# Weight folding in a four-layer attention kernel: 32-row block transposes through DRAM in place of TensorE transposes, rests gathered, weight reloads ordered behind a branch

## The chip, the cores and the metric

The kernel runs on one core of one Trainium2 chip. Its time is the device time of one execution in microseconds; of several executions the median counts. The profile shown is of one such execution.

## The reference, cut to what matters

Two kinds of layer alternate twice (A, B, A, B) on 2048 tokens of width D = 576 with 32 heads of 18. The same weights serve both rounds.

```python
def _A_ref(x, wq, wk, wv, wo):            # 32 query heads, one key and value head
    q = (x @ wq).reshape(B, S, H, Dh).transpose(0, 2, 1, 3)
    k = x @ wk; v = x @ wv
    p = softmax(einsum("bhqd,bkd->bhqk", q, k) * (Dh ** -0.5))
    return einsum("bhqk,bkd->bhqd", p, v) ... @ wo
def _B_ref(x, wqkv, w_phi, wo):           # linear attention
    q, k, v = (x @ wqkv) split
    pq = einsum("bhsd,hdf->bhsf", q, w_phi); pk = the same of k
    phi = concat(softmax(p), softmax(-p))            # for q and for k
    o = phi_q (phi_k^T v) / (phi_q sum(phi_k))
    return o ... @ wo
x = x + A(layernorm(x)); x = x + B(layernorm(x)); and both once more
```

`x @ wqkv` followed by the per-head product with `w_phi` is a product with a weight that can be worked out once: for queries and for keys, wq' = wq·blockdiag(w_phi). Working this out is called **folding** here.

## The kernel before, in words

One program does two rounds, "layer 0" and "layer 1", each an A and a B. The long stage of each round is `attend`. Its work is cut into 1024 **units**: for one of 32 groups (128 tokens, 16 heads), one of 16 key tiles and one of two halves of the heads, two score products on TensorE (L518) and one exponential of 128x1024 on ScalarE (L984). Two units make the weights of one key tile, which `add_values` (L796) multiplies with the values: that is called a **value step** here (8 matmul records). Units are done in **bursts** of three (`BURST`): six score records, then one, two or three value steps. A generator (`stream`) hands out **fills**, pieces of other TensorE work that are put into a burst, between its scores and its value steps (or instead of these): kind F for folding, P for one half of a projection of 128 tokens (L240, 14 records), U for a state update (L595). F and P fills each cost one credit; each burst earns `st["pace"]` credits, from `PACES`: in layer 0 0.6 while folding and 0.44 afterwards, in layer 1 0.39 throughout. When the generator has nothing (`idle`), units go by two with one value step. The stage's order on TensorE and VectorE is fixed as it is written (`in_order` chains these engines' instructions); on SyncE (SP, which issues nearly all DMAs) and ScalarE a scheduler decides. Every burst calls `tick` once or twice; a tick moves one step on in each of three queues: `urgent` (closing a group: `finish_group`, five VectorE steps and DMAs), `loads` (loading, splitting, saving weights) and `slow` (token transposes through DRAM).

In layer 0 `stream` first folds (`fold_phi`): ten slabs of wqkv, five for keys (half 1) and five for queries (half 0), 128 rows by 576 columns each. A slab takes three F fills: TensorE transposes its four blocks of 126 columns (L350, four records, copied to `wt` by VectorE, L351); the products with the block-diagonal `bd` (L355, eight records, copied by L357); and the product of the 72 columns that are left (L360, two records, copied by L362) together with the transpose of the next slab's 72 columns (L337, copied by L338). Results go to DRAM (`scratch`, tile `folded`), from where `load_weight` fetches them as the weights "wk" and "wpq". Then the **mix** begins: for tokens of layer B, projections to keys, values and queries, and state updates, tile by tile, until few units are left; three token tiles are done after the last unit. Layer 1 does the same without folding; its weights were saved to DRAM in layer 0 and are fetched again by `reload_weight` (L203) through the queue `loads`.

Ahead of the units 12 score units run for which a branch (L1007) decides whether they stand; each engine reads the flag (`TENSOR_LOAD safe`) and jumps over a block that is not run here.

Of the kernel before, what the change touches and what calls it, by code (L numbers as in the profile page):

```python
# [9 lines left out]
F32 = mybir.dt.float32  # L10
# [51 lines left out]
def kernel(ctx, tc, x_in, wq, wk, wv, wo, wqkv, w_phi, wob, out):  # L62
# [246 lines left out]
    def fold_phi(ps, tmp, pool):  # L309
        room = tmp("bd")  # L310
# [12 lines left out]
        wt, fo = tmp("wt"), tmp("fo")  # L323
        units = [(half, k) for half in (1, 0) for k in range(KT)]

        def fetch(n):
# [8 lines left out]
        def short(pl, st):  # L335
            if st is not None:
                T.transpose(pl[:72, :P], st[:, 504:576], idf)  # L337
                V.tensor_copy(wt[:72, 512:640], pl[:72, :P])  # L338

        slabs_in = deque(fetch(n) for n in range(3))  # L340
        yield STAGE
        yield STAGE
        pl = yield from bankful("F", ps, (P, P))
        short(pl, slabs_in[0])
        yield -110
        for n, (half, k) in enumerate(units):
            st = slabs_in.popleft()
            pt = yield from bankful("F", ps, (P, 4, P))
            for g in range(4):
                T.transpose(pt[:126, g, :], st[:, g * 126 : (g + 1) * 126], idf)  # L350
            V.tensor_copy(wt[:126, 0:512], pt[:126].rearrange("p a b -> p (a b)"))  # L351
            yield -440
            po = yield from bankful("F", ps, (P, 504))
            for g in range(4):
                T.matmul(po[:, g * 126 : (g + 1) * 126], wt[:126, g * P : (g + 1) * P],  # L355
                         bd[:126, g].rearrange("p a b -> p (a b)"), start=True, stop=True)
# [3 lines left out]
            T.matmul(pl[:, P : P + 72], wt[:72, 512:640],  # L360
                     bd[:72, 4, :4, :].rearrange("p a b -> p (a b)"), start=True, stop=True)
            V.tensor_copy(fo[:, 504:D], pl[:, P : P + 72])  # L362
            short(pl, slabs_in[0])
# [506 lines left out]
    def attend(layer, st, a1o, stream):  # L870
# [13 lines left out]
        with ctx1:  # L884
# [208 lines left out]
    PINNED = (mybir.EngineType.PE, mybir.EngineType.DVE)  # L1093
    DONE = object()

    class View:
# [117 lines left out]
    for layer in range(LAYERS):  # L1214
        last = layer == LAYERS - 1
        st.update(start_state(bw), added=set())
        with tc.tile_pool(name="a1o", bufs=2) as a1o:

            def load(key, place, *args, **kw):
                st[key] = weight_tiles(place) if isinstance(place, str) else place.weights()  # L1220
                yield from reload_weight(key) if key in wd else load_weight(st[key], *args, **kw)
# [13 lines left out]
            def stream(v, layer=layer):  # L1235
# [35 lines left out]
                if layer == 0:  # L1271
                    yield from wait(lambda: len(loads) > 0)
                    loads.extend((save_weight("wo"), save_weight("wq"), delayed(load_wv(), 5), load("wob", "a", wob, slice(0, D)),
                                  save_weight("wob")))

                    def room(name):
                        if name == "wt":
                            return bw.tile([P, 5 * P], F32, name="xn")
                        tag = {"fo": "featk", "bd": "featq"}[name]
                        return bw.tile([P, H, 2, DH], F32, name=tag).rearrange("p h s d -> p (h s d)")  # L1280

                    for step in fold_phi(ps, room, v.a1):
                        yield step
                        if finished and not isinstance(step, Kind) and (step is STAGE or step < 0):
                            yield from finish_tile()
                else:
                    loads.append(load_wv())
                loads.append(load("wk", "a", scratch[1], slice(0, D), padded=True))
                loads.append(load("wpq", "c", scratch[0], slice(0, D), padded=True))
                if layer == 0:  # L1290
                    st["saves"] = [save_weight(key) for key in ("wpq", "wk", "wv")]
                st["pace"] = PACES[layer][1]
                fetched = xs = None
                weights = False
# [224 lines left out]
```

## Time and profile before

| | us |
|---|---|
| median of three runs (2696.07 to 2699.16) | 2696.3 |
| profiled execution, its own time | 2694.4 |
| its span, first to last instruction | 2692.6 |
| TensorE (PE) busy | 2609.5 |
| ScalarE (ACT) busy | 2153.4 |
| VectorE (DVE) busy | 1239.0 |
| ACT, exponentials of the units (L984) | 1922.5 |

1.8 us lie outside the span. The exponentials of layer 0 start between 111.1 and 1228.6 us of the span, those of layer 1 between 1462.6 and 2541.4. What lies between and behind is the read-out of layer B and the queries of the next round. In a timeline row stand the start, the time from the first start to the last end of the merged records, the engine, the line, the operation, output and inputs, the number of records, and in brackets the idle time ahead of it with what ended it. Matmul records overlap, so the distance from one row's start to the next row's start is what a piece of work occupies.

### The profile page before, as it was taken

To read this page: it belongs to the slowest core of one execution; us is meant where nothing else is said; L and a number is where in the kernel's file an instruction comes from. 1 tells how busy PE (TensorE), PEld (TensorE's weight loads), DVE (VectorE), ACT (ScalarE), POOL (GpSimd) and SP (SyncE) were. 2 spreads that over 40 slices of the span, in tenths; PEclk is the share of its full clock that TensorE was granted. 3 is DMA by queue.
4 is the path that set the end of the run, shared out by engine and by line. 5 is a ranking of instruction groups with operands and counts; after the bars stand their busy time and mean duration, and the time that the engine had idled before them with its cause. 6 is when DMAs were issued, how large, how long until landed. Compare 5 with 4: busy or idle time off the path is not lost. (4 is left out here: it accounts for less than half of the span.)

```text
span 2692.6 us, 55535 instructions
## 1 busy us (share of the span) xinstructions
PE 2609.5 (97%) x22052; PEld 1444.7 (54%) x22052; DVE 1239.0 (46%) x2839; ACT 2153.4 (80%) x2529; POOL 66.2 (2%) x106
## 2 busy tenths in 40 slices
PE   7989999999999999999998999999999999999999
PEld 6633345554545544437997244444444444444498
DVE  8532244545445444435774124444444444444265
ACT  4588898998888889994334999999999999999821
POOL 1000000000000000001100000000000000000010
PEclk9999999999999999999999999999999999999999
DMA  5573134222233222224645412222222222222264
GB/s 183 155 238 117 50 116 125 70 67 57 55 68 73 59 47 57 56 64 135 201 148 165 146 50 59 59 59 59 59 59 59 56 54 57 56 58 57 50 194 140
DMA packets 469358, 245.06 MB, mean 91 GB/s; under 512 B 213410, under 2 KB 426850, under 8 KB 469090
## 3 DMA queue, kind: packets, MB, share of 16 engines
q1 hardware_dynamic: 467618, 238.46, 31.9%
q8 instruction: 177, 2.90, 0.5%
q10 hardware_dynamic: 1472, 2.95, 0.4%
q14 instruction: 91, 0.75, 0.1%
HBM read 133.86 MB, written 105.51 MB: 89 GB/s over the span
## 5 line engine op out<-in xcount | busy, mean ns | idle before, releaser
L984 ACT ACTIVATE pt<-sc 128x1024 f32<-128x1024 f32 x2036 | 1922.5, 1053 | 199.8 <-PE sc L518 179.8
L518 PE MATMUL sc<-qst,kst 56*128 56x512 f32 x3840 | 699.4, 452 | 26.5 <-ACT pt L984 26.2
L518 PEld LDWEIGHTS sc<-qst,kst 56*128 56x128 f32 x3840 | 320.1, 184 | 564.7 <-ACT pt L984 514.1
L796 PE MATMUL acc<-pt,vst 128*32 128x512 f32 x4096 | 499.9, 599 | 0.6 <-DVE featq L551 0.2
L796 PE MATMUL ps<-pt,vst 128*32 128x512 f32 x4048 | 486.1, 602 | 3.3 <-DVE featk L551 2.9
L796 PEld LDWEIGHTS ps<-pt,vst 128*32 128x32 f32 x4048 | 109.2, 110 | 231.2 <-issue 224.8
L796 PEld LDWEIGHTS acc<-pt,vst 128*32 128x32 f32 x4096 | 104.2, 109 | 211.4 <-issue 206.7
L304 DVE TENSOR_TENSOR xc<-xc,acc 128x288 f32<-128x288 f32 x60 | 27.2, 454 | 339.5 <-PE acc L240 339.5
L240 PE MATMUL ps<-wahi,xs 128*128 128x288 f32 x801 | 173.4, 302 | 3.1 <-ACT xs L131 1.9
L240 PEld LDWEIGHTS ps<-wahi,xs 128*128 128x128 f32 x801 | 130.8, 188 | 12.2 <-issue 3.1
L240 PE MATMUL ps<-walo,xs 128*128 128x288 f32 x445 | 130.3, 295 | 0.0
L240 PE MATMUL acc<-wdhi,on 128*128 128x288 f32 x540 | 119.7, 307 | 1.6 <-DMA on<-od 1.6
L240 PE MATMUL ps<-wchi,xs 128*128 128x288 f32 x504 | 111.2, 306 | 0.0
L396 PE MATMUL ps<-xsc,wbhi 128*128 128x256 f32 x576 | 106.9, 284 | 0.7 <-ACT xsc L131 0.7
L418 ACT ACTIVATE pc<-ps 128x256 fp32r<-128x256 f32 x80 | 30.5, 385 | 93.7 <-PE ps L396 90.9
L131 ACT ACTIVATE xs<-ps 128x512 fp32r<-128x512 f32 x36 | 21.4, 595 | 103.7 <-PE ps L290 103.7
L240 PEld LDWEIGHTS acc<-wdhi,on 128*128 128x128 f32 x540 | 87.9, 188 | 23.2 <-issue 20.5
L396 PEld LDWEIGHTS ps<-xsc,wbhi 128*128 128x128 f32 x576 | 90.7, 191 | 1.6 <-ACT xsc L131 1.1
L240 PEld LDWEIGHTS ps<-wchi,xs 128*128 128x128 f32 x504 | 82.3, 188 | 15.9 <-issue 14.2
L271 POOL TENSOR_TENSOR rstd<-var,neghalf 128x1 f32<-128x1 f32 (+1 forms) x56 | 32.1, 573 | 2382.5 <-DVE var L269 2359.9
L240 PE MATMUL acc<-wdlo,on 128*128 128x288 f32 x300 | 88.2, 294 | 0.0
L396 PE MATMUL ps<-xsc,wblo 128*128 128x256 f32 x320 | 85.7, 283 | 0.0
(269 smaller groups left out, 3032.6 us busy)
## 6 DMA issues: line engine op xcount, KB each, us to landing
qst<-qd SPq DMA_DIRECT2D x360, 72.0 KB
od<-parts SPq DMA_DIRECT2D x512, 36.0 KB
pht<-phi SPq DMA_DIRECT2D x32, 540.0 KB
qd<-pc SPq DMA_DIRECT2D x64, 256.0 KB
on<-od SPq DMA_DIRECT2D x60, 256.0 KB
phi<-pht SPq DMA_DIRECT2D x104, 144.0 KB
xd<-xc SPq DMA_DIRECT2D x33, 288.0 KB
flipped<-pht SPq DMA_DIRECT2D x112, 72.0 KB
```

Of the source, the lines that this page charges most:

```text
L131: A.activation(dst_hi, src, AF.Copy)
L240: T.matmul(dst, xs[:, slot, :], w[half][:, k, c0 : c0 + HALF], start=(n == 0), stop=(n == last))
L271: G.tensor_tensor(rstd, var, neghalf[:, :n], op=ALU.pow)
L304: V.tensor_add(xr, xr, po)
L396: T.matmul(po, lhs, xsc[:, slot, :], start=(n == 0), stop=(n == LASTP))
L418: A.activation(pc[:, 0, :], po, AF.Copy)
L518: T.matmul(sc, kst[head_rows(h), t * P : (t + 1) * P], q[head_rows(h), h // 2, :], start=True, stop=True)
L796: T.matmul(acc[32 * j : 32 * j + 32, :], vst[:, t, :], pts[j], start=first, stop=last)
L984: A.activation(pt, sc, AF.Exp, scale=SCALE)
```

## The change

Line numbers of the changed program are other ones: scores L553, value steps L831, block transposes through DRAM L686, folding products L384, products of the rests L394, token loads of the branch L1047.

- **Transposing.** A second generator, `turn`, is put into the queue `slow`. For each slab VectorE transposes 32x32 blocks within the slab (`block_transpose`, the function that the token tiles use already), four DMAs write the blocks to their places in DRAM (`turnedd`), one per tick, and two more DMAs fetch the transposed slab again: 504 columns to one of three buffers, the 72 that are left to `ends`. The 50 transposes of TensorE and their 20 copies are gone.
- **Folding.** A slab is one F fill, its four large products; it is put in once `ready` says that a later slab's load has been issued. The rests of the five slabs of a half are one fill: five products into one PSUM bank, one copy, one DMA.
- **Loads.** "wk" is put into `loads` when half 1 is done, "wpq" when half 0 is; before, both after the last slab.
- **Pace.** The mix of layer 0 gets 0.39 in place of 0.44.
- **Reloads.** In layer 1 each SP instruction of the queue `loads` is ordered behind the last TensorE instruction recorded so far, which is behind the branch.

```diff
+    def fold_phi(ps, pool, slow, folded):
...
+        wts = [wide[:, 0:512], wide[:, D : D + 512], spare[:, 0:512]]
+        ends = {1: spare[:, 512:], 0: bw.tile([P, KT * P], F32, name="xn")}
...
+        def load(n):
+            half, k = units[n]
+            wt = wts[n % len(wts)].rearrange("p (g t) -> p g t", t=P)
+            nc.sync.dma_start(wt[:126], turnedd[n, :504].rearrange("(g p) t -> p g t", p=126))
+            nc.sync.dma_start(ends[half][:72, k, :], turnedd[n, 504:])
+        def turn():
+            slabs = deque(fetch(n) for n in range(3))
+            for _ in range(3):
+                yield STAGE
+            for n in range(len(units)):
+                while n - done[0] > len(wts):
+                    yield STAGE
+                yield from block_transpose(blocks[n % 2], slabs.popleft(), turnedd[n])
+                slabs.append(fetch(n + 3))
+                if n:
+                    load(n - 1)
+                    ready[0] = n - 1
+                    yield STAGE
...
+        slow.append(turn())
         for n, (half, k) in enumerate(units):
-            st = slabs_in.popleft()
-            pt = yield from bankful("F", ps, (P, 4, P))
-            for g in range(4):
-                T.transpose(pt[:126, g, :], st[:, g * 126 : (g + 1) * 126], idf)
-            V.tensor_copy(wt[:126, 0:512], pt[:126].rearrange("p a b -> p (a b)"))
-            yield -440
+            while ready[0] <= n:
+                yield STAGE
             po = yield from bankful("F", ps, (P, 504))
             for g in range(4):
                 T.matmul(po[:, g * 126 : (g + 1) * 126], wt[:126, g * P : (g + 1) * P], ...)
-            V.tensor_copy(fo[:, :504], po)
+            V.tensor_copy(fo, po)
+            nc.sync.dma_start(scratch[half, k * P : (k + 1) * P, :504], fo)
             yield -880
-            pl = yield from bankful("F", ps, (P, 2 * P))
-            T.matmul(pl[:, P : P + 72], wt[:72, 512:640], ...)
-            V.tensor_copy(fo[:, 504:D], pl[:, P : P + 72])
-            short(pl, slabs_in[0])
-            slabs_in.append(fetch(n + 3))
-            nc.sync.dma_start(scratch[half, k * P : (k + 1) * P, :], fo[:, :D])
-            yield -330
+            if k == KT - 1:
+                pl = yield from bankful("F", ps, (P, KT * 72))
+                for j in range(KT):
+                    T.matmul(pl[:, j * 72 : (j + 1) * 72], ends[half][:72, j, :], ...)
+                V.tensor_copy(fo[:, : KT * 72], pl)
+                nc.sync.dma_start(scratch[half]...[:, :, 504:], ...)
+                folded(half)
+                yield -600
...
 def tick():
                 for queue in (urgent, loads, slow):
+                    begun = len(traced(nc))
                     if queue and next(queue[0], DONE) is DONE:
                         queue.popleft()
+                    if queue is loads and layer and PE in last:
+                        for i in traced(nc)[begun:]:
+                            if i.engine == mybir.EngineType.SP:
+                                tc.add_manual_dep(i, last[PE], NOSYNC, reason="order")
...
-    PACES = ((0.6, 0.44), (0.39, 0.39))
+    PACES = ((0.6, 0.39), (0.39, 0.39))
...
+                    def folded(half):
+                        key, place = ("wk", "a") if half else ("wpq", "c")
+                        loads.append(load(key, place, scratch[half], slice(0, D), padded=True))
```

TensorE in layer 0, in the middle of the first slabs. Before (`fstage` is the slab, `featq` holds `bd`, `xn` the transposed slab):

```order
L518 MATMUL sc<-xs,kst 128x512 x6
L360 MATMUL ps<-featq,xn 128x72
L337 MATMUL ps<-idf,fstage 72x128
L796 MATMUL ps<-pt,vst 32x512 x4
L518 MATMUL sc<-xs,kst 128x512 x6
L350 MATMUL ps<-idf,fstage 126x128 x4
L796 MATMUL acc<-pt,vst 32x512 x8
L518 MATMUL sc<-xs,kst 128x512 x6
L796 MATMUL acc<-pt,vst 32x512 x4
L518 MATMUL sc<-xs,kst 128x512 x6
L355 MATMUL ps<-featq,xn 128x126 x4
L796 MATMUL acc<-pt,vst 32x512 x8
```

After (`featx` and `xs` are the buffers that hold the transposed slab):

```order
L553 MATMUL sc<-xs,kst 128x512 x6
L384 MATMUL ps<-featq,featx 128x126 x4
L831 MATMUL acc<-pt,vst 32x512 x4
L553 MATMUL sc<-xs,kst 128x512 x6
L831 MATMUL acc<-pt,vst 32x512 x8
L553 MATMUL sc<-xs,kst 128x512 x2
L553 MATMUL sc<-qst,kst 128x512 x4
L384 MATMUL ps<-featq,featx 128x126 x4
L831 MATMUL acc<-pt,vst 32x512 x4
```

A slab's three fills became one; the whole of layer 0 has 31 F fills before and 12 after, and the first P fill of the mix stands 100 units earlier. In both programs 108 P fills and 13 U fills stand in a layer, and what is left for after its last unit is the same.

SP in layer 0, while the slabs are transposed; before there is nothing of this kind. After (rows with `turnedd` are new, `wstage` and `wqd` belong to the weight loads and saves that were there before):

```order
L686 DMA turnedd<-pht 32x18x32 x2
L168 DMA wstage<-in_B_wqkv_dram 128x576 x2
L686 DMA turnedd<-pht 32x18x32
L352 DMA featx<-turnedd 126x4x128
L353 DMA xs_2335<-turnedd 72x128
L686 DMA turnedd<-pht 32x18x32 x4
L168 DMA wstage<-in_B_wqkv_dram 128x576
L352 DMA featx<-turnedd 126x4x128
L353 DMA xs_2335<-turnedd 72x128
L168 DMA wstage<-in_B_wqkv_dram 128x576
L686 DMA turnedd<-pht 32x18x32
L389 DMA folded<-featk 128x504
```

The stores and loads of the transposed slabs stand in one queue with weight loads that wait for free staging buffers.

SP at the branch of layer 1. Before:

```order
L203 DMA wbhi<-wvd 128x576
L203 DMA wblo<-wvd 128x576
L1007 TENSOR_LOAD safe
L1007 ISA x2
L203 DMA wdhi<-wod 128x576
L203 DMA wdlo<-wod 128x576
```

Eight more reloads of these two kinds follow, and then the branch. After:

```order
L465 DMA kst<-pc 18x256 x5
L460 DMA qd_104<-pc 128x2x256 x4
L483 DMA mxd_106<-length 32x256
L1047 TENSOR_LOAD safe
L1047 ISA x2
L537 DMA qst<-qd_104 18x8x128 x6
L1047 COMPARE_AND_BRANCH
```

Fourteen reloads of 288 KB (four of "wv", ten of "wo") left the place ahead of the branch, and six query loads of 72 KB, which stood behind it, took it.

More of the change, by code (lines that the diff above doesn't have):

```diff
@@ L322, in fold_phi @@
         yield STAGE
-        wt, fo = tmp("wt"), tmp("fo")
+        outs = flat_room("featk")
+        outs = [outs[:, n * D : n * D + 504] for n in range(2)]
+        wide = flat_room("featx")
+        spare = bw.tile([P, 9, P], F32R, name="xs2").bitcast(F32).rearrange("p a b -> p (a b)")
+        wts = [wide[:, 0:512], wide[:, D : D + 512], spare[:, 0:512]]
+        ends = {1: spare[:, 512:], 0: bw.tile([P, KT * P], F32, name="xn")}
+        ends = {half: t.rearrange("p (k t) -> p k t", t=P) for half, t in ends.items()}
+        blocks = bw.tile([P, NKG, P], F32, name="pht").rearrange("p a b -> p (a b)")
+        blocks = [blocks[:, n * 5 * P : n * 5 * P + D] for n in range(2)]
         units = [(half, k) for half in (1, 0) for k in range(KT)]
+        ready, done = [0], [0]
         def fetch(n):
@@ L333, in fetch @@
             return st
[L335 to L343, printed above, removed]
-        short(pl, slabs_in[0])
-        yield -110
-        for n, (half, k) in enumerate(units):
-            st = slabs_in.popleft()
-            pt = yield from bankful("F", ps, (P, 4, P))
-            for g in range(4):
-                T.transpose(pt[:126, g, :], st[:, g * 126 : (g + 1) * 126], idf)
-            V.tensor_copy(wt[:126, 0:512], pt[:126].rearrange("p a b -> p (a b)"))
-            yield -440
+        def load(n):
[16 more added lines that the diff above has]
+                    yield STAGE
+            for _ in range(2):
+                yield STAGE
+            load(len(units) - 1)
+            ready[0] = len(units) - 1
+            for _ in range(5):
+                yield STAGE
+            ready[0] = len(units)
+        slow.append(turn())
+        slot = 0
+        for n, (half, k) in enumerate(units):
+            while ready[0] <= n:
+                yield STAGE
             po = yield from bankful("F", ps, (P, 504))
+            wt = wts[n % len(wts)]
             for g in range(4):
@@ L1274, in stream @@
                                   save_weight("wob")))
[L1276 to L1282, printed above, removed]
+                    def folded(half):
+                        key, place = ("wk", "a") if half else ("wpq", "c")
+                        loads.append(load(key, place, scratch[half], slice(0, D), padded=True))
+                    for step in fold_phi(ps, v.a1, slow, folded):
                         yield step
@@ L1285, in stream @@
                             yield from finish_tile()
+                    st["saves"] = [save_weight(key) for key in ("wpq", "wk", "wv")]
                 else:
                     loads.append(load_wv())
[L1288 to L1291, printed above, removed]
+                    loads.append(load("wk", "a", scratch[1], slice(0, D), padded=True))
+                    loads.append(load("wpq", "c", scratch[0], slice(0, D), padded=True))
                 st["pace"] = PACES[layer][1]
```

19 lines of the change are left out of this document (13 added, 6 removed).

## The prediction

> **What bounds the kernel now.** The page first: TensorE is busy for nearly all of the span.
>
> ```profile
> span 2692.6 us, 55535 instructions
> PE 2609.5 (97%) x22052; PEld 1444.7 (54%) x22052; DVE 1239.0 (46%) x2839; ACT 2153.4 (80%) x2529; POOL 66.2 (2%) x106
> ```
>
> A busy share is an average, so next comes the view of the exponentials' line, once for each layer (count, shortest, median and longest in ns, first and last start).
>
> ```profile
> L984 ACT ACTIVATE pt<-sc x1018: 1007/1027/1392, 116.6 to 1228.6; 128x1024 f32<-128x1024 f32 x170
> L984 ACT ACTIVATE pt<-sc x1018: 1004/1027/1588, 1468.0 to 2541.4; 128x1024 f32<-128x1024 f32 x170
> ```
>
> The same 1018 exponentials take 1112.0 us in layer 0 and 1073.4 us in layer 1. Layer 0 has the folding and the higher pace; layer 1 has neither, so it serves as a measured model of layer 0 without them. Next, TensorE's timeline inside the folding:
>
> ```profile
> 242.76 0.44 PE L360 MATMUL ps<-featq,xn 72*128 72x72 f32 x2
> 243.53 0.30 PE L337 MATMUL ps<-idf,fstage 128*72 128x128 f32 x1 [0.33 <-DVE featk L362]
> 243.76 1.92 PE L796 MATMUL acc<-pt,vst 128*32 128x512 f32 x16
> ...
> 249.74 0.66 PE L350 MATMUL ps<-idf,fstage 128*126 128x128 f32 x4
> 250.32 1.93 PE L796 MATMUL acc<-pt,vst 128*32 128x512 f32 x16
> 252.18 0.97 PE L518 MATMUL sc<-qst,kst 56*128 56x512 f32 x6
> ...
> 255.69 0.49 PE L518 MATMUL sc<-qst,kst 56*128 56x512 f32 x2 [0.41 <-ACT pt L984]
> 256.12 1.92 PE L796 MATMUL ps<-pt,vst 128*32 128x512 f32 x16
> 257.97 0.96 PE L518 MATMUL sc<-qst,kst 56*128 56x512 f32 x6
> ```
>
> Three things are to be seen. Two bursts without a fill, 252.18 to 257.97, take 5.79 us for six units, and TensorE waits for ScalarE in them (0.41 us). The fills occupy 1.00 us (L360 with L337, a third of it waiting for VectorE's copy) and 0.58 us (L350). And a fill is paid or not according to the burst that it falls in:
>
> ```profile
> 282.06 0.49 PE L518 MATMUL sc<-qst,kst 56*128 56x512 f32 x2
> ...
> 284.11 1.16 PE L355 MATMUL acc<-featq,xn 126*128 126x126 f32 x8
> ...
> 287.05 0.96 PE L518 MATMUL sc<-qst,kst 56*128 56x512 f32 x6
> ...
> 288.94 0.50 PE L518 MATMUL sc<-qst,kst 56*128 56x512 f32 x2
> 302.08 0.97 PE L518 MATMUL sc<-qst,kst 56*128 56x512 f32 x6
> 302.98 1.16 PE L355 MATMUL ps<-featq,xn 126*128 126x126 f32 x8
> ...
> 305.06 1.03 PE L518 MATMUL sc<-qst,kst 56*128 56x512 f32 x6
> ...
> 307.88 0.73 PE L518 MATMUL sc<-qst,kst 56*128 56x512 f32 x4
> ```
>
> In a burst with two value steps the folding product costs 6.88 − 5.79 = 1.09 us over a plain pair (282.06 to 288.94); in one with a single value step the pair takes 5.80 (302.08 to 307.88), so it costs nothing. Bound here is neither engine alone but the handing over between them.
>
> **Layer 0, stage by stage.** I sum the changed layer 0 from the burst at 148.75 us, where the first folding fill of before stands; up to it the order on TensorE is the same. By the order's counts 985 units follow there. Their prices:
>
> ```profile
> 148.75:1229.50 1080.75, 931.14 (x986) 0.99 0.30 80
> 1598.70:2542.50 943.80, 841.14 (x890) 1.00 0.24 58
> ...
> 1534.27 0.91 PE L518 MATMUL sc<-qst,kst 56*128 56x512 f32 x4
> ...
> 1536.11 0.91 PE L518 MATMUL sc<-qst,kst 56*128 56x512 f32 x4
> ...
> 1605.37 0.97 PE L518 MATMUL sc<-qst,kst 56*128 56x512 f32 x6
> ...
> 1608.32 1.06 PE L518 MATMUL sc<-qst,kst 56*128 56x512 f32 x6
> ...
> 1612.03 0.73 PE L518 MATMUL sc<-qst,kst 56*128 56x512 f32 x4
> ```
>
> The first two rows are stretches of ScalarE's work on the units (length, busy, count). Before, the stretch takes 1228.6 − 148.75 = 1079.9 us. After:
> 1. 18 plain units until the first slab is ready: 3 × 5.79 = 17.4.
> 2. 78 units with the folding, 13 pairs × 5.79 = 75.3. Of the 12 fills six stand in bursts with one value step (0) and six in bursts with two or three: 6 × 1.09 = 6.5. Two P fills of the first output tile: a pair with one takes 6.66 (1605.37 to 1612.03), 0.87 more, 1.7 together. Sum 83.5.
> 3. 20 units while weights and tokens arrive: 14 in idle pairs at 1.84 (1534.27 to 1536.11), 12.9, and 6 plain, 5.8 to 6.4. Sum 19.
> 4. The mix to the last unit, 869 units with 106 P and 13 U fills. Layer 1's stretch from 1598.7 holds the same fills and 889 units in 2541.4 − 1598.7 = 942.7; its 20 units more are idle ones at 0.92, 18.4. So 924.3.
>
> Sum 1044.2, or **35.7 us less**. The cheaper pace needs no term of its own, since stage 4 is priced at layer 1's pace; nothing is pushed behind the last unit, where the order stands as before.
>
> What the sum leaves out are waits. Before has these, and after loses the first two, which stand in the 1079.9:
>
> ```profile
> 185.38 0.43 PE L337 MATMUL acc<-idf,fstage 128*72 128x128 f32 x1 [3.97 <-DVE featk L362]
> 295.99 0.30 PE L337 MATMUL ps<-idf,fstage 128*72 128x128 f32 x1 [1.81 <-DVE featk L362]
> 966.60 4.29 PE L796 MATMUL ps<-pt,vst 128*32 128x512 f32 x24 [2.85 <-DVE featk L551]
> 180.00:190.00 10.00, 6.03 (x31) 2.66 (x27) 6.53 (x14) 4.83 (x6) 0.00 (x0) 0.73 0.55 176
> ```
>
> All three are TensorE held by VectorE's queue. The last row, a window with 0.73 as its granted clock, shows that a stall of 4 us is followed by a slow clock, so that it costs more than itself; at 966.60 three value steps take 4.29 us, where two take 1.92 (256.12). The Trainium skill ("TensorE: Matmul & The Clock Gate", Part 1) says the same: a window of about 3.4 us of idleness halves the clock. By it a wait below that is cheap, and the 1.81 us one would cost only itself; I hold the row of 966.60 against this, where 2.85 us sufficed.
>
> New waits: TensorE's folding product waits for a load behind four stores behind a VectorE transpose, all in SP's one queue, and everything behind it on TensorE waits too, scores included. VectorE itself is eased: ten transposes at 0.78 against 30 copies.
>
> ```profile
> L646 DVE STREAM_TRANSPOSE pht<-xc x28: 778/778/781, 370.3 to 2463.4; 128x576 f32<-128x576 f32 x28
>   DVE xs L133: 3.6, 1
> 190.00:200.00 10.00, 10.00 (x71) 3.94 (x70) 2.50 (x4) 7.98 (x10) 0.00 (x0) 0.93 1.00 336
> ```
>
> The middle row is from the view of the tile `flipped`, by which the tokens of the mix go the same way in both layers: of all 28 only one was waited for, 3.6 us. The DMA engines are full at times in this stretch (share 1.00 at 336 GB/s), and 5.9 MB more go through them there: at that rate 17.6 us spread over 85. A load is issued some five ticks ahead of its product; four ticks go into a pair of bursts (5.79 us), so about 7 us. The lower bound of the waits is 0, as it is for 27 of the 28 token tiles. The upper bound for the likely case is the 185.38 wait twice with its slow clock, 2 × 6 = 12. I take 4, nearer to 0 because of the five ticks, and 2 more for one bunching as at 966.60 where the phases of mix and groups shift: **−30**. The skill ("DMA: Bandwidth & Descriptors", Specifications) names 512 bytes as the least run for the full rate and a read-modify-write below it; the stores here have runs of 128 bytes. If that halved their rate (my estimate from it), the 17.6 would be 26, still a third of the stretch; no row here separates these stores.
>
> **The branch of layer 1.**
>
> ```profile
> 123.24 1.14 PE L518 MATMUL sc<-wclo,kst 56*128 56x512 f32 x6 [0.85 <-DMA featq<-in_B_w_phi_dram]
> 1480.15 1.84 PE L518 MATMUL sc<-wclo,kst 56*128 56x512 f32 x6 [6.21 <-SPq L1007]
> L1007 PEldq COMPARE_BRANCH  x2: 451/3676/6902, 121.1 to 1472.3; - x2
> 1467.11 0.32 SPq L203 DMA_DIRECT2D wdhi<-wod  x1
> ...
> 1471.68 0.73 SPq L203 DMA_DIRECT2D wdlo<-wod  x1
> ```
>
> At the first layer's branch TensorE loses 0.85 us, at the second 6.21: its own branch instruction takes 6.90 us from 1472.3, right behind ten reloads (1467.11 to 1472.4). Two readings: it fetches code through DMA engines that are full, or the fetch is slow in itself. By the first and with free engines the gain is 5.4, and 2.2 more since the six scores behind it take 1.84 instead of 1.14 and slow value steps follow: 7.6. But after, SP reaches its branch some 3 us earlier than TensorE its own, and the same reloads then stand right behind it; so they may fill the engines at 1472 all the same. The gain lies between 0 and 7.6; I take **2**, near the lower end. The skill ("Runtime: NRT & Kernel Launch", Instruction fetch mechanics) says that a taken branch out of the fetched window forces a fetch by DMA before anything runs; it speaks for the price at 1472.3, but not for the 0.45 us of the first branch.
>
> Sum: 2694.4 − 30 − 2 = 2662.4 for such a profiled execution; the median shown is 1.9 above it, so **2664**.
>
> **The rivals.**
> - *Moderate waits.* Five of the 12 folding products wait like the one at 295.99, 1.8 us and about 1 of slow clock each: 14 in place of 4 + 2, so −24 instead of −32, and with bunching once more −20: **2676**. For it: full DMA engines at 190 to 200. Against: the five ticks.
> - *Slower: the fold's round trip through SP.* If SP falls behind, each product waits as at 185.38, 4 us and 2 of slow clock. Against a gain of 38 without any waits (35.7 + 2) it decides from about six such waits; with all 12, 72 us, the result is 2696.3 − 37.7 + 72 = **2731**. For it: stores and loads stand among weight loads that wait for staging buffers. Against: the one wait among the 28 token tiles.
> - *No change.* The transposes lay in time that TensorE had free anyway, and ScalarE sets the end: then the pairs with L350 and L360 would take 5.79 like plain ones. The rows above contradict this for the fills (a third of the 1.00 us is waiting). **2696**.
>
> **How the numbers follow.** Forecast 0.67 (2664, its own range 2653 to 2672), moderate waits 0.21, no change 0.04, slower 0.08. The range takes in the fast bound (35.7 + 7.6 = 43, 2653, a little below for the bounds of stage 3) and the moderate waits with their spread: 2650 to 2684. 0.2%, 5.4 us, is about what a measurement can tell from no change: faster 0.88, same 0.04, slower 0.08.
>
> **What would show it.** Right: layer 0's 1018 exponentials span about 1080 us instead of 1112; pairs of bursts around the folding at 5.8 or 6.9; the first P fill of the mix near 268 us; the same rows from there as in layer 1. Wrong: waits of L384 or L394 on a DMA over 1 us, a clock below 1 in windows between 160 and 250, an idle stretch of TensorE longer than 20 us ahead of the mix, or the three-step bursts of the mix over 3.8 us. For the branch, TensorE's branch instruction: under 1 us, or near 6.9 again.

## The result, and the profile after

The changed kernel takes 2685.53 us (median of 5 runs, 2683.45 to 2686.72) against 2696.3 (2695.05 to 2699.16): 0.996 of the time, 95% interval 0.995 to 0.9971. That is 10.8 us less, where 32 less were forecast; it lies 1.5 us above the range. The profiled execution has a span of 2684.3 us, 8.3 less than that of before: the profiled execution of before lay 1.9 us below its median, this one (2686.1) lies 0.6 above its own.

Where the 8.3 us come from is read from the exponentials' line, as ahead of the change: count, shortest, median and longest in ns, first and last start.

```profile
L1024 ACT ACTIVATE pt<-sc x1018: 1005/1026/1422, 117.5 to 1222.7; 128x1024 f32<-128x1024 f32 x170
L1024 ACT ACTIVATE pt<-sc x1018: 1003/1027/1588, 1462.4 to 2533.1; 128x1024 f32<-128x1024 f32 x170
```

Layer 1 spans 1070.7 us, 2.7 less. Layer 0 spans 1105.2 instead of 1112.0, only 6.8 less; its first start lies 0.9 us later than before, so the two parts come to more than 8.3. The same view, cut after the first 129 exponentials of layer 0 (128 units), shows that these 6.8 are a gain and a loss. First the kernel before, then the changed one:

```profile
L984 ACT ACTIVATE pt<-sc x129: 1017/1030/1181, 116.6 to 257.3; 128x1024 f32<-128x1024 f32 x129
```

```profile
L1024 ACT ACTIVATE pt<-sc x129: 1017/1032/1192, 117.5 to 280.4; 128x1024 f32<-128x1024 f32 x129
```

The first 128 units take 162.8 us (from the unrounded starts) instead of 140.7: **22.1 lost**. They hold all of the changed kernel's folding, but not all of the folding before, which goes on to 351 us. The other 889 units take 942.4 (280.4 to 1222.7) instead of 971.2: **28.8 gained**. These two stretches are the measure of every experiment below.

Who waits in the first stretch is shown by TensorE's timeline; the brackets hold the wait ahead of a row and what ended it. L384 is the folding product, eight instructions a slab, so a row is one fill.

```profile
175.05 2.05 PE L384 MATMUL ps<-featq,featx 126*128 126x126 f32 x8 [6.64 <-DMA featx<-turnedd]
183.05 1.16 PE L384 MATMUL ps<-featq,featx 126*128 126x126 f32 x8
197.06 2.08 PE L384 MATMUL acc<-featq,xs 126*128 126x126 f32 x8 [5.16 <-DVE turned L933]
224.69 1.13 PE L384 MATMUL acc<-featq,featx 126*128 126x126 f32 x8 [0.62 <-DMA featx<-turnedd]
250.36 2.08 PE L384 MATMUL ps<-featq,featx 126*128 126x126 f32 x8 [9.77 <-DVE featk L388]
```

Three of the ten products stand still, 21.6 us together, and each then runs at half speed, 2.05 to 2.08 us against 1.13 to 1.16. The windows show the slow clock behind them (length; busy time and count of PE, PEld, DVE, ACT, POOL; granted clock; DMA share; GB/s):

```profile
170.00:180.00 10.00, 4.95 (x23) 2.67 (x23) 3.72 (x6) 1.19 (x2) 0.00 (x0) 0.66 0.83 201
190.00:200.00 10.00, 4.43 (x26) 2.62 (x26) 4.70 (x9) 4.10 (x5) 0.00 (x0) 0.65 0.76 198
200.00:210.00 10.00, 9.37 (x61) 3.03 (x54) 5.69 (x11) 6.29 (x7) 0.00 (x0) 0.84 0.54 138
250.00:260.00 10.00, 9.02 (x51) 4.39 (x52) 6.16 (x11) 4.15 (x5) 0.00 (x0) 0.78 0.73 184
```

In each row the busy time of PE times what the granted clock lacks of 1 is an estimate of what the slow clock cost: 1.7 + 1.6 + 1.5 + 2.0 = 6.8 us. Stalls and slow clock come to 28 us.

Only the first stall ends with a reload's landing. The other two end with VectorE, and the view of waits says for what VectorE itself stood between 140 and 270 us (total, times, longest):

```profile
DVE wahi L133 <- DMA wstage<-folded: 13.4, 2, 13.1
DVE pht L681 <- DMA turnedd<-pht: 12.8, 2, 12.4
DVE wahi L133 <- DMA wstage<-in_B_wo_dram: 12.4, 2, 8.7
```

L133 is the cast that begins the split of a weight. The cast of wob at the head of VectorE's fixed order holds `finish_group`'s transpose behind it, and that holds the product at 197; the cast of wk holds the copy of a product (L388), and that the product at 250. Why the loads land late is seen in SP's queue, where each row is one or several issues:

```profile
163.68 0.32 SPq L197 DMA_DIRECT2D wqd<-wblo  x1
...
165.61 1.18 SPq L686 DMA_DIRECT2D turnedd<-pht  x2
166.84 1.05 SPq L168 DMA_DIRECT2D wstage<-in_B_wqkv_dram  x2
167.93 0.43 SPq L686 DMA_DIRECT2D turnedd<-pht  x1
172.07 0.34 SPq L352 DMA_DIRECT2D featx<-turnedd  x1
```

and in SP's own waits between 140 and 210:

```profile
SPq L197 <- DMA fstage<-in_B_wqkv_dram: 10.7, 3, 5.7
...
SPq L544 <- DMA fstage<-in_B_wqkv_dram: 3.8, 1, 3.8
SPq L352 <- DMA fstage<-in_B_wqkv_dram: 3.7, 1, 3.7
```

The first reload (172.07) stands behind saves of wq (wqd), stores and wv's loads; and SP stands 18.2 us with a slab load (fstage) named as the releaser, though ScalarE's queue issues the slabs and SP's instructions use none of their data. The kernel before has such waits too, 13.4 us between 120 and 300, but no product there waited for a reload.

At layer 1's branch:

```profile
L1047 PEldq COMPARE_BRANCH  x2: 358/2700/5042, 122.0 to 1466.7; - x2
1472.47 1.57 PE L553 MATMUL sc<-wclo,kst 56*128 56x512 f32 x6 [3.96 <-DMA wdhi<-wod]
```

TensorE's branch takes 5.04 us instead of 6.90, and the scores behind it wait 3.96 instead of 6.21.

### The profile page after: what moved, and what is told of

It is laid out like the page before. It is cut to its first block, busy times and chain, and to the rows that moved or that the text cites. A ratio compares the mean times of both kernels' runs of the same rounds, so it can differ in the third digit from the quotient of the medians.

```text
span 2684.3 us, 55497 instructions
## 1 busy us (share of the span) xinstructions
PE 2601.8 (97%) x22002; PEld 1441.9 (54%) x22002; DVE 1235.8 (46%) x2821; ACT 2153.7 (80%) x2529; POOL 66.0 (2%) x106
## 5 line engine op out<-in xcount | busy, mean ns | idle before, releaser
L553 PE MATMUL sc<-qst,kst 56*128 56x512 f32 x3840 | 697.7, 451 | 21.4 <-ACT pt L1024 20.9
L553 PEld LDWEIGHTS sc<-qst,kst 56*128 56x128 f32 x3840 | 318.3, 184 | 561.5 <-ACT pt L1024 511.9
L831 PE MATMUL acc<-pt,vst 128*32 128x512 f32 x4096 | 499.7, 601 | 0.6 <-DVE featk L586 0.4
L831 PE MATMUL ps<-pt,vst 128*32 128x512 f32 x4048 | 485.3, 601 | 0.0
L831 PEld LDWEIGHTS ps<-pt,vst 128*32 128x32 f32 x4048 | 108.8, 109 | 226.6 <-issue 224.8
L831 PEld LDWEIGHTS acc<-pt,vst 128*32 128x32 f32 x4096 | 105.0, 109 | 214.1 <-issue 211.3
L240 PE MATMUL ps<-wahi,xs 128*128 128x288 f32 x729 | 158.3, 303 | 2.3 <-ACT xs L131 1.9
L240 PEld LDWEIGHTS ps<-wahi,xs 128*128 128x128 f32 x729 | 120.3, 190 | 7.6 <-issue 2.7
L240 PE MATMUL acc<-wdhi,on 128*128 128x288 f32 x540 | 119.6, 306 | 0.0
L240 PE MATMUL ps<-walo,xs 128*128 128x288 f32 x405 | 119.3, 297 | 0.0
L240 PE MATMUL ps<-wchi,xs 128*128 128x288 f32 x531 | 117.1, 306 | 0.0
L240 PEld LDWEIGHTS acc<-wdhi,on 128*128 128x128 f32 x540 | 88.0, 187 | 21.2 <-issue 19.7
L240 PEld LDWEIGHTS ps<-wchi,xs 128*128 128x128 f32 x531 | 86.6, 188 | 17.0 <-issue 16.5
L240 PE MATMUL acc<-wahi,xs 128*128 128x288 f32 x423 | 94.0, 307 | 0.4
L586 DVE COPY featk<-acc 128x288 f32<-128x288 f32 x47 | 21.4, 456 | 153.1 <-PE acc L240 152.8
```

Of the source, the lines that this page charges most:

```text
L240: T.matmul(dst, xs[:, slot, :], w[half][:, k, c0 : c0 + HALF], start=(n == 0), stop=(n == last))
L553: T.matmul(sc, kst[head_rows(h), t * P : (t + 1) * P], q[head_rows(h), h // 2, :], start=True, stop=True)
L586: V.tensor_copy(e[:, hs, 0, :], src)
L831: T.matmul(acc[32 * j : 32 * j + 32, :], vst[:, t, :], pts[j], start=first, stop=last)
```

## The experiments

Theory: the missing 22 us are the three stalls in the folding with the slow clock behind them, and they come from SP's one queue, either directly (a reload issued late) or through VectorE's fixed order (a split whose load was issued late). Rivals: packets of 128 bytes fill the DMA engines; the cheaper order on TensorE is worth less than summed; or the gain comes from the pace or the branch. Each kernel is measured against the kernel before, run again beside it. The columns are the two stretches of layer 0, layer 1, and the median. The stretches come from one profiled execution each; in e1, e9, e10 and e12 that was the slowest one, 2.8 to 3.4 us above its median.

| kernel | first 128 units | other 889 | layer 1 | median, us |
|---|---|---|---|---|
| before | 140.7 | 971.2 | 1073.4 | 2695.2 to 2696.5 |
| changed | 162.8 | 942.4 | 1070.7 | 2685.53 |
| e1 | 141.2 | 973.3 | 1072.1 | 2692.42 |
| e2 | 152.0 | 948.1 | 1070.8 | 2681.55 |
| e3 | 158.5 | 942.2 | 1070.2 | 2680.42 |
| e4 | 144.1 | 966.9 | 1069.6 | 2690.21 |
| e5 | 154.1 | 942.3 | 1070.6 | 2677.60 |
| e6 | 158.0 | 942.2 | 1072.1 | 2688.83 |
| e7 | 149.8 | 942.3 | 1070.3 | 2680.53 |
| e8 | 164.6 | 953.4 | 1069.9 | 2695.51 |
| e9 | 148.9 | 942.2 | 1072.0 | 2670.85 |
| e10 | 148.3 | 945.1 | 1071.7 | 2673.51 |
| e11 | 164.2 | 942.1 | 1070.8 | 2687.17 (one run) |
| e12 | 141.6 | 942.7 | 1071.9 | 2663.68 |
| e13 | 158.0 | 942.7 | 1070.5 | 2680.64 |
| e14 | 141.0 | 971.3 | 1072.7 | 2694.62 |

**e1, the branch alone.** On the kernel before:

```diff
+                    begun = len(traced(nc))
                     if queue and next(queue[0], DONE) is DONE:
                         queue.popleft()
+                    if queue is loads and layer and PE in last:
+                        for i in traced(nc)[begun:]:
+                            if i.engine == mybir.EngineType.SP:
+                                tc.add_manual_dep(i, last[PE], NOSYNC, reason="order")
```

> The kernel before with one part of the change alone: the reloads of layer 1 are held behind the matmuls of their place. Theory (the parts add up): layer 0 is the same to 0.5 us, layer 1's exponentials span 1073.4 - 2.7 = 1070.7 us as in the changed kernel, the time is 2693.6. Rival (the 2.7 us came from elsewhere, from the folding's DMAs that are gone by then or from another place of the branch in a fetch window): layer 1 stays at 1073.4 and the time at 2696.3.

2692.42 us, 0.9989 (0.9979 to 0.9998), so the time is on the side of the theory. In the trace layer 1 gets 1.3 us shorter, not 2.7, and layer 0 is 2.4 longer instead of the same, so single executions of this order differ by that much. In the other kernels with this edit layer 1 is 1.3 to 3.8 shorter than before; in e14, which lacks it, 0.7. The part is small and uneven.

**e8, the pace alone taken back.**

```diff
-    PACES = ((0.6, 0.39), (0.39, 0.39))
+    PACES = ((0.6, 0.44), (0.39, 0.39))
```

> The changed kernel with the pace of the mix of layer 0 at 0.44, as before, in place of 0.39. If the lower pace is worth nothing by itself (the prediction gave it no term): 2683 to 2688, with the stretch to 290 us the same. If it is what keeps VectorE from bunching as at 966.60 in the kernel before: layer 0's slices of 32 units in the mix rise from 34.2 to 35.2 us on average, some 20 us, 2700 to 2706.

2695.51 us, 1.0003 (0.9993 to 1.0012): without the pace the whole change is worth nothing. The other 889 units take 953.4 us, 11.0 more than at 0.39, so of the 28.8 us gained there 11.0 go with the pace and 17.8 with the fills that are gone. Most of the 17.8 does not lie where those fills stood: behind unit 320 neither kernel folds, and there e8 takes 746.9 us and the kernel before 761.8. The mix starts earlier in e8, so fewer of its P fills are left there (1148 records of L240 against 1274). Both expectations missed; the pace counts, for half of what the second said. The pace alone on the kernel before was not tried, so what it is worth there is not shown.

**e3, long runs.** The block stores write 32 runs of 2304 bytes:

```diff
-            nc.sync.dma_start(dst[:, rows].rearrange("(b f) t -> f b t", f=32), ...)
+            nc.sync.dma_start(whole[rows], blocks[rows, :])
```

> The changed kernel, whose block stores write the same bytes in the same 40 instructions, but in runs of 2304 bytes and not of 128; so the folded weights are those of a slab in another order of elements. Theory (SP's queue and VectorE's fixed order make the stalls: the stores' number and place in the queue): stalls at 175, 197 and 250 stay within 20%, 2680 to 2687. Rival (the stores' 576 packets of 128 bytes each fill the DMA engines, and loads land late behind them): the share of the DMA engines in 150 to 260 falls from 0.76 to below 0.6, the three stalls go, 23 us and some 4 of slow clock: 2659.

2680.42 us, 0.9946 (0.9929 to 0.9962). The stalls are 4.18, 5.15 and 7.08 us, 16.4 in place of 21.6; two of them fall by more than the 20% that the theory allowed. The window of the first stores, of the changed kernel and then of e3:

```profile
150.00:170.00 20.00, 16.57 (x118) 5.34 (x114) 2.35 (x4) 19.23 (x22) 0.00 (x0) 1.00 0.82 243
```

```profile
150.00:170.00 20.00, 16.26 (x114) 5.09 (x112) 2.42 (x4) 19.24 (x22) 0.00 (x0) 1.00 0.81 264
```

At the same share of the DMA engines 264 instead of 243 GB/s are moved. So the short runs cost 4 to 5 us, and the three stalls, which the rival would see gone, remain. The Trainium skill ("DMA: Bandwidth & Descriptors", Specifications) names 512 bytes as the least transfer for the full rate; the two rows agree that shorter runs lose rate, but only a quarter of the stalls hangs on it here.

**e11, reloads that wait for no store.**

```diff
-            nc.sync.dma_start(wt[:126], turnedd[n, :504].rearrange("(g p) t -> p g t", p=126))
-            nc.sync.dma_start(ends[half][:72, k, :], turnedd[n, 504:])
+            cols = slice(half * D + k * 64, half * D + k * 64 + P)
+            nc.sync.dma_start(wt[:126], wqkv[:504, cols].rearrange("(g p) t -> p g t", p=126))
+            nc.sync.dma_start(ends[half][:72, k, :], wqkv[504:, cols])
```

> The changed kernel, whose reloads read the same number of bytes from the weights in DRAM and not from the stored slabs, so that they stand at their places in SP's queue but wait for no store; the products then multiply other numbers. Theory (the reload is late because SP reaches it late, behind saves and loads): the stall at 175 stays between 5 and 8 us. Rival (the reload is issued in time and waits for its four stores to land): the stall falls under 1.5 us.

```profile
175.14 2.05 PE L385 MATMUL ps<-featq,featx 126*128 126x126 f32 x8 [7.34 <-DMA featx<-in_B_wqkv_dram]
```

The stall stays, though the reload needs no store now. The rival is ruled out; layer 0 is 1106.3 us, as without the edit.

**e2, wk's load behind the last slab**, as in the kernel before.

```diff
-                        key, place = ("wk", "a") if half else ("wpq", "c")
-                        loads.append(load(key, place, scratch[half], ...))
+                        if not half:
+                            loads.append(load("wk", "a", scratch[1], ...))
+                            loads.append(load("wpq", "c", scratch[0], ...))
```

> The changed kernel, with the load of wk put behind the last slab as before, not behind the fifth. Theory (three stalls, each with a cause of its own; the one of 9.77 us ahead of 250.36 is VectorE held at the split of wk, whose load SP issued late): that stall goes, 9.8 us and some 3 of slow clock, the other two stay: 2673. Rival A (the folding as a whole is short of DMA, and a stall goes only to come back as another wait for a reload): 2682 to 2688. Rival B (wk now ends later and the mix starts later; units wait idle at 0.92 us, which costs nothing): no loss, so this agrees with the theory.

2681.55 us, 0.9951 (0.9934 to 0.9968). The stall at 250 goes (products wait 0.43 us at most there), and the first 128 units fall by 10.8, close to the 9.8 + 3 expected. But behind them 5.7 come back, a stall of 3.37 us at 298.9 among them, where a split of wpq holds VectorE in front of an output tile. The theory is right about this stall; the total (2673 by the theory) falls just below rival A's 2682 to 2688.

**e4, no split while slabs are folded.** wv, wob and wk are all loaded behind the last slab.

```diff
-                    loads.extend((save_weight("wo"), save_weight("wq"), delayed(load_wv(), 5), load("wob", ...),
-                                  save_weight("wob")))
+                    loads.extend((save_weight("wo"), save_weight("wq")))
...
+                        if not half:
+                            loads.extend((load_wv(), load("wob", ...), save_weight("wob"), load("wk", ...), load("wpq", ...)))
```

> The changed kernel, with the loads of wv and wob, the save of wob and the load of wk all behind the last slab, so that no weight is split on VectorE while slabs are folded; the saves of wo and wq stay where they were. Theory (VectorE's fixed order is held at splits whose loads are late): the stalls at 197 and 250 go, 15 us and 4 of slow clock, that at 175 (a reload behind saves) stays or shrinks: 2662 to 2668, less what a later mix costs, which I put at 0 to 5. Rival (short of DMA bandwidth whatever the order): fold products wait for reloads at other places, 2678 to 2686.

2690.21 us, 0.9979 (0.9969 to 0.9988), a miss. The first 128 units fall by 18.7, as the theory has it; products wait 2.20 us at most. The others take 966.9, 24.5 more: the mix begins at 333.2 instead of 313.7, and splits of wob now stand in VectorE's order ahead of an output tile (5.58 us at 293.2). So the gain in the folding is lost again behind it. Some 10 of the 24.5 us lie in the next 128 units; the rest is spread over the mix, and its cause is open.

**e5, splits later.** The loads stay where they are; the first split of a weight follows five ticks behind.

```diff
-                    ..., load("wob", "a", wob, slice(0, D)),
+                    ..., delayed(load("wob", "a", wob, slice(0, D)), 5),
-                        loads.append(load(key, place, ...))
+                        loads.append(delayed(load(key, place, ...), 5))
```

> The changed kernel, with five ticks between the first loads and the first split of wob, wk and wpq, as wv has them already; the amounts that move are the same. Theory (VectorE's fixed order stands at splits whose loads have not landed): the stalls of 5.2 us at 197 and of 9.8 us at 250 go, and 4 of slow clock with them; that of 6.6 us at 175 stays. Layer 0 falls from 1105 to 1086, the time to 2666; weights that are ready later may give back up to 8. Rival (the DMA engines are short, whoever waits): VectorE's or TensorE's waits for DMA between 150 and 300 sum to no less than before, 2680 to 2688.

2677.60 us, 0.9938 (0.9921 to 0.9954). The stalls at 197 and 250 fall to 1.42 and 1.76 us, and that at 175 stays at 7.06: through which engine each stall comes is shown. The time falls by 8 and not by 19: 2.35 and 0.88 us come up in an output tile (waiting for its `on`, again a load of SP's) and the product that waits 1.76 us still runs at half speed.

**e6, wq saved early**, in the setup of the first layer; **e7**, e5 and e6 together.

```diff
             clear_shifts()
             yield STAGE
+            run(save_weight("wq"))
...
-                    loads.extend((save_weight("wo"), save_weight("wq"), ...
+                    loads.extend((save_weight("wo"), ...
```

> The changed kernel, whose split wq is saved while the queries of the first layer are still made (between 20 and 110 us, where the DMA engines are busy to 0.4), and not beside the first two slabs. Theory (the stall at 175 is the first reload standing behind ten saves of 288 KB): it falls from 6.6 us to under 1, with 2 of slow clock; the other two stay within 2 us: 2677. Rival (the first reload is late because of the slab's own four stores of 128-byte runs): the stall stays over 4 us, 2682 to 2686.

> The changed kernel with both edits, the splits five ticks later and wq saved early. If the three stalls are all that the prediction missed, layer 0 spans 1105 - 21.6 - 6 = 1077 us and the time is 2658, up to 2668 where one new stall of VectorE comes up in the mix; if a stall taken away comes back at the next place that is short of DMA, 2672 to 2682.

e6: 2688.83 us, 0.9971 (0.9959 to 0.9984); e7: 2680.53, 0.9943 (0.9927 to 0.996). The first product waits 0.90 us, as the theory has it; the next one waits 3.21. In e7 the first 128 units are down to 149.8. But the first exponential starts at 126.1 and 126.4 instead of 117.5: the ten saves now stand at 34 to 41 us in SP's queue, ahead of the queries' own DMAs, and the stage before ends 9 us later. Neither expectation had this: e6 lies above both of its ranges, and e7 in that of the stall that comes back elsewhere (2672 to 2682).

**e9, wq saved ahead of the stores.** On e5; the save of wo moves behind the folding, which puts the save of wq ten instructions earlier.

```diff
-                    loads.extend((save_weight("wo"), save_weight("wq"), ...
+                    loads.extend((save_weight("wq"), ...
-                    st["saves"] = [save_weight(key) for key in ("wpq", "wk", "wv")]
+                    st["saves"] = [save_weight(key) for key in ("wo", "wpq", "wk", "wv")]
```

> The kernel with five ticks ahead of the first splits, and with the save of wo moved behind the folding, so that the save of wq comes ten instructions earlier in SP's queue, ahead of the first slab's stores and not among them; nothing is added to the stages before. Theory (the stall of 7.06 us ahead of the first product is the first reload behind saves of 288 KB): it falls to under 1.5 us, layer 0 from 1096.3 to 1088, the time from 2677.6 to 2669. Rival (it moves to the next products, as where wq was saved early): waits of products for reloads still sum to over 4 us between 165 and 200, 2674 to 2679.

2670.85 us, 0.9902 (0.9886 to 0.9919). The first product, which waited 7.06 us, waits no more, as the theory has it; but now the second one waits 3.75 us, as the rival has it, and 2.97 and 2.57 us come up in an output tile at 202 and 205. The time is near the theory's, 6.8 less than e5's.

**e10, the same at a pace of 0.38.**

> The same with a pace of 0.38 in layer 0. From 0.44 to 0.39 the pace was worth 12.8 us of layer 0 (1117.9 against 1105.2). If that goes on in proportion, 2.5 us less than the same kernel at 0.39; if at 0.39 all idle units were used up already, the same within 1 us; if the fills no longer end in time, more behind the last unit.

2673.51 us, 0.9913 (0.9896 to 0.993): 2.7 more than e9, and the two intervals overlap. The gain of the lower pace doesn't go on, and none of the three expectations fits: the other 889 units take 945.1, with a new stall of 2.06 us at 1083.

**e12, slabs through SP's queue**, on e9. **e13**, the same edit alone on the changed kernel. **e14**, on the kernel before.

```diff
-                nc.scalar.dma_start(st[r, :], part)
+                nc.sync.dma_start(st[r, :], part)
```

> The kernel with the later splits and wq's save ahead of the stores, whose slabs of the folding are loaded through SP's queue and not ScalarE's. In the trace of that kernel SP stands 21 us between 140 and 210 with a slab load on ScalarE's queue named as what released it, five times 3.3 to 4.8 us. Theory (SP's standing still on those loads is what makes the remaining reloads and splits late): SP's waits named after the slabs fall under 3 us, the gap of 3.75 us at 178.7 under 1.5, those of 3.0 and 2.6 us at 202 and 205 under 1.5 together; layer 0 from 1091 to 1082, the time 2662 to 2664. Rival (SP stands because the DMA engines have not finished earlier work, whoever issued it): the waits stay and are named after other transfers, 2668 to 2674.

2663.68 us, 0.9879 (0.9861 to 0.9896), the fastest kernel of all. SP's longest waits between 140 and 210 now:

```profile
SPq L863 <- DVE parts L133: 14.4, 2, 12.5
SPq L352 <- PE sc L553: 1.1, 2, 0.7
```

and on TensorE's timeline the one stall over 1 us that is left in the folding:

```profile
234.61 2.04 PE L384 MATMUL ps<-featq,featx 126*128 126x126 f32 x8 [4.08 <-DMA featx<-turnedd]
```

The waits named after slab loads are down to 0.5 us in all; what is left is SP standing for `parts`, which VectorE makes (14.4 us, 7.6 in e9). The gaps at 178.7, 202 and 205 are gone, and the time is the theory's; layer 0, 1084.3, is 2 us over it, with the new stall of 4.08.

> The changed kernel with one edit only: the slabs of the folding are loaded through SP's queue and not ScalarE's. In its own trace SP stands 18 us between 140 and 210 with a slab load named as what released it. Theory (these standstills are the root of the three stalls, and the other edits only moved things out of their reach): the stalls at 175, 197 and 250 fall from 21.6 us to under 8, layer 0 from 1105 to 1088 or less, the time to 2668 or less. Rival (three causes side by side, saves, splits and slabs, each good for a third): layer 0 falls by 5 to 8, the time is 2677 to 2681.

> The kernel before with the same edit: slabs through SP's queue. Its TensorE transposes wait for slabs alone and for nothing that SP reloads. Theory (SP's standing still costs only where something near on TensorE's path comes back through SP): the same within 3 us of 2696. Rival (it costs any order): 5 to 15 us less.

e13: 2680.64 us, 0.9934 (0.9917 to 0.995), so the theory of one root fell. The stalls are 4.82, 1.87 and 9.88 us: the one at 197 falls from 5.16 to 1.87, that at 175 by a quarter, that at 250 is untouched. Saves, splits and slabs act side by side, and e12 has an edit for each. e14: 2694.62, 0.9992 (0.9982 to 1.0001), the same as before: SP's standing still costs nothing where no product comes back through SP.

## Why the prediction was wrong

1. **The price of the order without waits was right.** Stage 4 was priced by layer 1 (942.7 us less idle units). By the prediction's terms the 889 units from the 128th on come to 19 + 924.3 = 943.3; measured are 942.4, and 942.1 to 942.7 in eight other kernels at a pace of 0.39; only where weights are loaded later (e2, e4) are there more. Of the 28.8 us gained there, 11.0 go with the pace (e8); a term of its own was not needed, but without the pace the result would have been no change.
2. **The failing step is the sum of new waits, "I take 4", and "2 more for one bunching".** By the prediction's terms the first 128 units take 133.1 us (32.2 to the burst at 148.75, 17.4 and 83.5), and 137.1 with the 4 of waits. They took 162.8: 21.6 us of stalls and some 7 of slow clock, which leaves 1 us open. The bunching in the mix did not come.
3. **Why 4 was taken.** "I take 4, nearer to 0 because of the five ticks": the ticks are counted in the program's order, but SP came to the first reload only at 172.07, behind saves (e6, e9) and after standing for slab loads (e12, e13); e11 shows that the place in the queue decides and not the stores. The row of the 28 token tiles, one wait in all, came mostly from stretches in which no weights go through SP.
4. **What was not thought of:** the path by VectorE. "VectorE itself is eased" is true of its work (1235.8 against 1239.0 us), but its order is fixed, and two of three stalls came through it (e2, e5). The row at 185.38, which the prediction read as TensorE held by VectorE's queue, was a sign of this path.
5. **The rivals.** Moderate waits (five of 1.8 us, 2676) had the size of loss too small and the waits too many: it was three of 5 to 10 us. The slower rival had the right mechanism, SP's queue, with three products hit instead of six or more, each at some 9 us instead of 6.
6. **The branch.** Forecast 2, between 0 and 7.6; measured 2.7, and 1.3 to 3.8 in all kernels with the edit. On the whole layer 1 gains the more, the shorter TensorE's branch is: 1.3 us at a branch of 5.60 (e1), 3.8 at one of 4.02 (e4). That SP's reloads would still stand there is borne out: the wait that is left ends with a reload (`wdhi<-wod`).
7. **A smaller miss:** the first product of the mix stands at 313.7, not near 268. That it stands later cost nothing there: in e12 it stands at 291.7, and the 889 units take 942.7.

e12 takes 2663.68 us where 2664 was forecast, but in its profiled execution (2666.57) the first 128 units take 141.6 and not 133.1 to 137.1; one stall of 4.08 us is shown there, with some 2 of slow clock behind it by the prediction's price, and the rest is open. That the totals agree is partly chance.

## What to carry to other kernels

When work moves from a busy engine to a round trip through DRAM, don't price the transfer: walk the issuing queue from the reload backwards and list what stands ahead of it, saves and loads of other stages included, and then walk the order of the engine that consumes it. A wait behind the head of a fixed order costs everything behind it, so leave several ticks between a load and the first instruction that needs it, as the e5 edit does. And sum a change in two stretches, with and without the moved stage: one number for both hides a gain of 28.8 behind a loss of 22.1.

## What the hardware showed

- **A wait of 1.75 us can halve the clock.** Over the changed kernel and twelve experiments, 12 folding products behind a wait of 0.42 to 1.42 us took 1.13 us each, and 27 behind one of 1.75 to 10.0 us took 1.83 to 2.08; the prediction's row of 966.60 (2.85) agrees. The two that lie next to this step in one kernel, e5:

```profile
191.96 1.13 PE L384 MATMUL acc<-featq,xs 126*128 126x126 f32 x8 [1.42 <-DMA xs<-turnedd]
...
246.74 2.05 PE L384 MATMUL ps<-featq,featx 126*128 126x126 f32 x8 [1.76 <-DMA featx<-turnedd]
```

  The length of the wait alone does not decide. The first record of an output tile ran at full clock behind a wait of 2.97 us in e9 (0.37 us), and at half clock behind one of 2.20 us in e7 (0.58). The row of e9 stands first:

```profile
202.18 0.37 PE L240 MATMUL acc<-wdhi,on 128*128 128x288 f32 x1 [2.97 <-DMA on<-od]
212.48 0.58 PE L240 MATMUL acc<-wdhi,on 128*128 128x288 f32 x1 [2.20 <-DMA on<-od]
```

  In e9 the granted clock was 1.00 from 202.0 to 202.9 us and 0.50 from 203.0 to 209.8. In the changed kernel it was 0.50 from 172.6 to 179.3, while its first product ran from 175.05: it fell during the wait and came back several us after TensorE had gone on. The Trainium skill ("TensorE: Matmul & The Clock Gate", Part 1) gives about 3.4 us of idleness; shorter waits were enough here, and the measurement decides.
- **A queue can stand for another queue's loads.** SP stood 18.2 us between 140 and 210 with slab loads named that ScalarE's queue issued; when SP issued them, those waits were 0.5 us (e12). What ties the two queues together no trace here shows.
- **TensorE's taken branch** took 4.0 to 5.6 us at layer 1 in the kernels with the dependency, 6.90 (before) and 6.78 (e14) without, against 0.36 to 0.45 at layer 0's branch, which no reloads precede. Full DMA engines alone do not explain it: in the kernel before their share was 0.97 at layer 0's branch (121.1 to 121.6 us), which took 0.45. Why the other one is slow stays open.
